# Sending sixteen rows of the first keys ahead of the weights in a GQA decode kernel

## The chip, the cores and the metric

The kernel runs on one core of one Trainium2 chip. The core has five engines that run side by side: TensorE (PE, matmuls; its weight loads are listed apart as PEld), VectorE (DVE), ScalarE (ACT), GpSimd (POOL) and SyncE (SP), and sixteen DMA engines that bring data from the chip's memory (HBM) to the on-chip memory of 128 partitions. The metric is the device time of one execution in microseconds, here the median of several runs. A profile of one execution goes with it; its span runs from the first to the last instruction.

## The reference

One decode step for 8 sequences: the sum of the input, an attention with grouped queries over a cache, and a dense layer with Mish. All data is float32.

```python
xn = _layernorm(x)                                   # x: 8 x 1 x 512
q = (xn @ wq) -> 32 heads of 128                     # wq: 512 x 4096
k, v: 8 x 8 key/value heads x 8192 positions x 128   # four query heads share one
p = softmax(q k^T * 128 ** -0.5);  o = p v
A = o @ wo                                           # wo: 4096 x 512
h = xn @ w1 + b1;  act = h * tanh(softplus(h))       # w1: 512 x 1792
out = x + A + act @ w2                               # w2: 1792 x 512
```

The two caches are 268 MB each; the weights together are some 24 MB. Each byte of a cache is used once.

## The kernel before

The work is cut in 16 packs (`PACKS`): a pack is a pair of key/value heads for two of the eight sequences (`PB`). For each pack and sequence there is one load of keys and one of values, 8 MiB each: 128 rows, one for each partition, of 64 KiB. The host lays the arrays out so that a load is one contiguous stretch of HBM; `rows_of` cuts it into 128 rows.

For each load of keys, PE multiplies it with the expanded queries (`scores`, 64 matmuls into bank `c`); ACT copies the result, PE arranges it in rows, DVE and ACT do the softmax, and one pack later PE multiplies the weights with the values (`values`, into bank `o`). Before all packs there is a part that runs once: `setup` (layer norm of x, small selector tables), `queries` (PE: xn times the first wq, then DVE scales and transposes) and `mish` (xn times w1, then a chain on DVE).

Three places on the chip take the large loads: "a" (tile `kva`, 64 KiB per partition), "b" (`kvb`, 80 KiB) and "w" (`kvw`, 16 KiB). `plan` (line 499) puts a load with its place in a list, `queue`; `pump` (479) takes loads from the head of that list as long as the place of the first one is free, and `release` (491) frees a place when its readers are done and pumps again. So the loads are issued strictly in the order of that list, all of them by SP on one DMA queue. x and b1, both small, are issued by ACT on its own queue. The calls that fill the list are on lines 545 to 571: the first is wq, the second w1 (to place "a"), the third the first keys (to place "b"); then come the second keys (to "a", so after w1's readers), and so on. The first three have places that are free at the start, so SP issues them one after another with no wait.

Each load has a stream, which is the semaphore that its landing raises (`"k0"` for the first keys). Which waits an instruction needs is worked out by `Program` from the tiles that it reads and writes: an instruction on PE that reads a tile written by a load waits for that load's semaphore, with one wait for each semaphore. In the profile nearly all instructions carry line 383, where `issue` emits them, so they are told apart by their tiles: `kvw<-in_wq` is the load of wq, `kva<-in_w` that of w1, `kvb<-in_kT` and `kva<-in_kT` those of keys, `h<-kvw,xnT` the query matmuls, `o<-kva,aT` the first matmuls of mish, `c<-kvb,qT` the scores.

```python
def pump():
    while queue and taken.get(queue[0][1]) in (None, queue[0][0]):
        what, at, load = queue.pop(0)
        taken[at] = what
        landed[what] = load()
```

Of the kernel before, what the change touches and what calls it, by code (L numbers as in the profile page):

```python
# [58 lines left out]
W1R = 2 * CC * P // P  # L59
W2R = G * FT // 2 * FP // P  # L60
FAR = 1e38


ENGINES = ("tensor", "vector", "scalar", "gpsimd", "sync")
# [379 lines left out]
def kernel(  # L444
# [14 lines left out]
    pe, dve, act, pool, sp = (getattr(prog, e) for e in ("tensor", "vector", "scalar", "gpsimd", "sync"))  # L459

    def tile_of(shape, name):
        prog.on_chip.add(name)
        return nc.alloc_sbuf_tensor(name, list(shape), F32).ap()
# [8 lines left out]
    queue = []  # L472
    taken, landed, held = {}, {}, {}

    def rows_of(blocks):

        return blocks.rearrange("j p f -> (j p f)").rearrange("(p f) -> p f", p=P)
# [18 lines left out]
            held[at] = [relay]  # L496
        pump()

    def plan(what, at, blocks, stream, part=(0, 1), lo=0):

        rows = rows_of(blocks)
        n = rows.shape[1]
        t = place[at][:, lo : lo + n]

        cols = slice(round(part[0] * n), round(part[1] * n))

        def load():
            sp.dma_start(t[:, cols], rows[:, cols], stream=stream, to="tensor", after=held.pop(at, ()))
            return t

        queue.append((what, at, load))

    sc = tile_of([P, 512], "sc")
    x_sb = sc[:B, :]
# [6 lines left out]
    def blocks_of(src, p, b):  # L521
        i, k = divmod(p, NP)
        lo = ((k * PB + b) * HKV + 2 * i) * NB
        return src[lo : lo + KN]

    up = [0]

    def plan_k(p, b):
        blocks = blocks_of(kT, p, b)
        if (p, b) == (0, 1):  # L530
            plan(("k", p, b), "a", blocks, "k1")
        else:
            up[0] = KX * BW - up[0]
            plan(("k", p, b), "b", blocks, "k" if p else "k0", lo=up[0])

    def plan_v(p, b, at, stream="v", part=(0, 1)):
        plan(("v", p, b), at, blocks_of(v, p, b), stream, part)

    def plan_wq(i):
        plan(("wq", i), "w", wq[i * CC : (i + 1) * CC], "w")  # L540
# [1 line left out]
    def plan_wo(i, stream="w", part=(0, 1)):  # L542
        plan(("wo", i), "w", wo[i * 4 : i * 4 + 4], stream, part)

    plan_wq(0)
    plan("w1", "a", w1, "w1")
    between = {}
    for i in range(1, PAIRS):
        between[NP * i - 1, 0] = ("wq", i)
# [1 line left out]
    for p in range(PACKS):  # L551
        for b in range(PB):
            plan_k(p, b)
            if (p, b) in between:
                what, i = between[p, b]
                (plan_wq if what == "wq" else plan_wo)(i)
            if p == 1 and b == 0:
                plan_v(0, 0, "a", "v1", (1 / 2, 1))
                plan_v(0, 0, "a", part=(0, 1 / 2))
            elif p > 0:  # L560
                plan_v(p - 1, b, "a")
# [65 lines left out]
    def setup():  # L627
# [63 lines left out]
        dve.reduce_sum(isel, rsel.rearrange("p (i r) -> p i r", i=W4), axis=AX.X)  # L691
        dve.tensor_scalar(far, isel, FAR, -FAR, op0=ALU.mult, op1=ALU.add)
        of_head = tile_of([P, 2, V8], "of_head")
# [365 lines left out]
    for p in range(PACKS):  # L1059
        prog.enter(p)  # L1060
        for b in range(PB):
            k = landed.pop(("k", p, b))
# [44 lines left out]
    p = PACKS - 1  # L1107
# [75 lines left out]
```

## Time and profile before

| what | value |
|---|---|
| median of 3 runs | 1303.62 us (1303.54 to 1303.68) |
| span of the profiled execution | 1302.2 us |
| PE, DVE, ACT, POOL busy | 67%, 30%, 9%, 0% of the span |
| moved by DMA | 561.22 MB, mean 431 GB/s |
| SP's queue (q1) | 99.7% of the 16 engines' span |
| first issue of SP, first score matmul | 0.74 us, 37.66 us |

The profiled execution lies 1.4 us below the runs, because the span leaves out what is before its first and behind its last instruction; its own time is its span beside that. The share of a DMA queue is the time that its packets took, summed over the sixteen engines and divided by sixteen times the stretch; it can pass 100% in a short stretch, because a packet is counted whole where it starts. One packet is one row of a load on one engine, and each load adds one packet of 4 bytes per engine that it runs on, for the semaphore.

### The profile page before, as it was taken

To read this page: it belongs to the slowest core of one execution; us is meant where nothing else is said; L and a number is where in the kernel's file an instruction comes from. 1 tells how busy PE (TensorE), PEld (TensorE's weight loads), DVE (VectorE), ACT (ScalarE), POOL (GpSimd) and SP (SyncE) were. 2 spreads that over 40 slices of the span, in tenths; PEclk is the share of its full clock that TensorE was granted. 3 is DMA by queue.
4 is the path that set the end of the run, shared out by engine and by line. 5 is a ranking of instruction groups with operands and counts; after the bars stand their busy time and mean duration, and the time that the engine had idled before them with its cause. 6 is when DMAs were issued, how large, how long until landed. Compare 5 with 4: busy or idle time off the path is not lost.

```text
span 1302.2 us, 11363 instructions
## 1 busy us (share of the span) xinstructions
PE 869.0 (67%) x4814; PEld 278.5 (21%) x4814; DVE 389.9 (30%) x597; ACT 122.2 (9%) x294; POOL 4.8 (0%) x10
## 2 busy tenths in 40 slices
PE   4786666766567665686656686666866656756568
PEld 1222112212112221122211222111221121212113
DVE  6350504305051230521405132052320515105061
ACT  1020202001020100200102020020100102001020
POOL 1000000000000000000000000000000000000000
PEclk9898789887799788897877897778877888878779
DMA  9999999999999999999999999999999999999998
GB/s 404 447 419 446 421 441 429 431 439 429 439 429 441 425 443 423 436 433 431 439 429 439 420 450 425 441 425 441 429 431 439 429 439 429 441 425 439 427 429 372
DMA packets 11554, 561.22 MB, mean 431 GB/s; under 512 B 1292, under 2 KB 1424, under 8 KB 1688
## 3 DMA queue, kind: packets, MB, share of 16 engines
q1 hardware_dynamic: 11520, 561.06, 99.7%
q8 instruction: 7, 0.11, 0.0%
q10 hardware_dynamic: 24, 0.02, 0.0%
q14 instruction: 3, 0.02, 0.0%
HBM read 561.01 MB, written 0.07 MB: 431 GB/s over the span
## 4 chain that ended last, share of the span: by engine, by line
DMA 61%; PE 31%; DVE 1%; issue 0%; SPq 0%; ACT 0%; DVEq 0%
DMA kvb<-in_kT 60%; PE c L383 29%; DMA kvb<-in_w 2%; PE o L383 1%; DVE raw L383 0%; DVE pt L383 0%; PE h L383 0%; DVE os L383 0%; DVE nm L383 0%; PE s L383 0%; PE m L383 0%; SPq L383 0%; ACT sc L383 0%; DVE acc L383 0%; DVE nr L383 0%
## 5 line engine op out<-in xcount | busy, mean ns | idle before, releaser
L383 PE MATMUL c<-kvb,qT 128*64 128x512 f32 x1984 | 497.7, 665 | 332.8 <-DMA kvb<-in_kT 332.2
L383 PEld LDWEIGHTS c<-kvb,qT 128*64 128x64 f32 x1984 | 160.8, 154 | 669.6 <-issue 459.4
L383 PE MATMUL o<-kva,pt 128*32 128x512 f32 x1984 | 238.0, 635 | 24.5 <-DMA kva<-in_v 24.1
L383 DVE TENSOR_REDUCE nm<-s 128x1 f32<-128x1024 f32 x16 | 19.6, 1225 | 437.0 <-PE s L383 437.0
L383 DVE STREAM_TRANSPOSE raw<-wide 128x2048 f32<-128x2048 f32 x36 | 125.5, 3485 | 19.5 <-ACT wide L383 17.7
L383 ACT COPY sc<-c 128x512 f32<-128x512 f32 x32 | 18.8, 586 | 979.1 <-PE c L383 979.1
L383 PEld LDWEIGHTS o<-kva,pt 128*32 128x32 f32 x1984 | 64.6, 116 | 189.1 <-issue 147.6
L383 ACT ACTIVATE wide<-s,nms 128x512 f32<-128x512 f32 x128 | 88.0, 688 | 130.4 <-DVE nms L383 66.9
L383 DVE TENSOR_TENSOR oT<-m,rt 128x16 f32 (+1 forms) x17 | 3.0, 175 | 229.6 <-PE m L383 229.6
L383 DVE TENSOR_SCALAR os<-o,isel 128x128 f32<-128x128 f32 x32 | 11.2, 350 | 151.1 <-PE o L383 151.1
L383 DVE TENSOR_TENSOR pt<-raw 64x256 f32<-64x256 f32 x128 | 53.6, 418 | 1.9
L383 DVE TENSOR_TENSOR qT<-qc,bsel 128x1024 f32<-128x1024 f32 x34 | 40.2, 1221 | 13.3 <-PE s L383 13.3
L383 PE MATMUL s<-sc,csel 64*128 64x512 f32 x128 | 37.1, 656 | 8.5 <-ACT sc L383 7.1
L383 DVE TENSOR_TENSOR raw<-raw 128x1024 f32<-128x1024 f32 x32 | 39.2, 1225 | 2.9 <-DVE raw L383 0.2
L383 DVE SCALAR_TENSOR_TENSOR os<-o,isel,os 128x128 f32<-128x128 f32 x96 | 33.6, 350 | 3.4
L383 ACT ACTIVATION_READ_ACCUMULATOR wide<-s,nms 128x1 f32 x128 | 24.7, 193 | 0.0
L383 PE MATMUL m<-hsel,os 128*128 128x8 f32 x66 | 12.7, 265 | 10.5 <-DVE lsel L383 10.5
L383 PE MATMUL m<-ident,nm 128*1 128x128 f32 x16 | 4.3, 270 | 21.6 <-DVE nm L383 21.6
L383 PE MATMUL h<-kvw,xnT 128*64 128x512 f32 x64 | 17.6, 700 | 0.0
L383 PE MATMUL c<-kva,qT 128*64 128x512 f32 x64 | 15.7, 652 | 2.1 <-DMA kva<-in_kT 2.1
L383 DVE TENSOR_SCALAR wide<-h 128x512 f32<-128x512 f32 x16 | 11.1, 691 | 19.9 <-PE h L383 19.5
L383 PEld LDWEIGHTS m<-hsel,os 128*128 128x128 f32 x66 | 10.1, 193 | 25.3 <-issue 12.2
(92 smaller groups left out, 162.1 us busy)
## 6 DMA issues: line engine op xcount, KB each, us to landing
kvw<-in_wq SPq DMA_DIRECT2D x4, 2048.0 KB, 30.3
kva<-in_v SPq DMA_DIRECT2D x2, 4096.0 KB, 21.6
kvw<-in_wo SPq DMA_DIRECT2D x3, 2048.0 KB, 30.4
kva<-in_v SPq DMA_DIRECT2D x1, 6144.0 KB, 24.3
kva<-in_w SPq DMA_DIRECT2D x1, 3584.0 KB, 15.8
kva<-in_v SPq DMA_DIRECT2D x1, 2048.0 KB, 28.8
kvb<-in_w SPq DMA_DIRECT2D x1, 2048.0 KB, 13.7
kvw<-in_wo SPq DMA_DIRECT2D x1, 1536.0 KB, 16.9
```

The costliest lines, as they stand in the source:

```text
L383: got = getattr(engine, o.method)(*args, **kw)
```

## The change

`plan` gets an argument `first`: the load that is put in the list then covers only the rows from `first` on, and the rows before it are issued at once, as a DMA of their own with a stream of its own, when `plan` is called. For the first keys `first` is 16. The calls for wq and w1 move behind the call for the first keys, and the rest of the first keys is taken from the head of the list to its end, so that the list begins with wq, w1, keys as before. SP's order of issue is then: rows 0 to 15 of the first keys (16 partitions, 1 MiB), wq, w1, the other 112 rows of the first keys (7 MiB). All other loads stand as they were.

```diff
+AHEAD = 16
...
-    def plan(what, at, blocks, stream, part=(0, 1), lo=0):
+    def plan(what, at, blocks, stream, part=(0, 1), lo=0, first=0):
...
         def load():
-            sp.dma_start(t[:, cols], rows[:, cols], stream=stream, to="tensor", after=held.pop(at, ()))
+            sp.dma_start(t[first:, cols], rows[first:, cols], stream=stream, to="tensor", after=held.pop(at, ()))
             return t
 
         queue.append((what, at, load))
+        if first:
+            sp.dma_start(t[:first], rows[:first], stream=stream + "a", to="tensor")
...
-            plan(("k", p, b), "b", blocks, "k" if p else "k0", lo=up[0])
+            plan(("k", p, b), "b", blocks, "k" if p else "k0", lo=up[0], first=0 if p else AHEAD)
...
-    plan_wq(0)
-    plan("w1", "a", w1, "w1")
     between = {}
...
     for p in range(PACKS):
         for b in range(PB):
             plan_k(p, b)
+            if p == b == 0:
+                plan_wq(0)
+                plan("w1", "a", w1, "w1")
+                queue.append(queue.pop(0))
```

## The prediction

> **What bounds the kernel now.** I read the page first: the busy shares, the strip of forty slices, the queues and the chain that ended last.
>
> ```profile
> PE 869.0 (67%) x4814; PEld 278.5 (21%) x4814; DVE 389.9 (30%) x597; ACT 122.2 (9%) x294; POOL 4.8 (0%) x10
> ...
> DMA  9999999999999999999999999999999999999998
> ...
> DMA packets 11554, 561.22 MB, mean 431 GB/s; under 512 B 1292, under 2 KB 1424, under 8 KB 1688
> ...
> q1 hardware_dynamic: 11520, 561.06, 99.7%
> ...
> DMA 61%; PE 31%; DVE 1%; issue 0%; SPq 0%; ACT 0%; DVEq 0%
> ```
>
> Queue q1, SP's own, carries 561.06 MB and keeps the 16 DMA engines at work for 99.7% of the span. PE's 31% of the chain is a way of following it back: while PE works, the transfers go on. The same view cut to the middle, 38 to 1170 us, leaves out both ends:
>
> ```profile
> DMA packets 9211, 490.26 MB, mean 433 GB/s; under 512 B 1024, under 2 KB 1024, under 8 KB 1024
> ...
> q1 hardware_dynamic: 9208, 490.21, 100.1%
> ```
>
> No gap at all. One engine moves 490.21 MB / 16 / 1132 us = 27.1 GB/s, so **a 64 KiB row takes 2.42 us**, and a load of 128 such rows (8 on each engine) 19.4 us. Nothing can catch up on a queue that is never idle: each microsecond in which an engine of the 16 moves less at the start comes back at the end. So the change is priced at the start of this queue alone. The end of the chain shows the transfers still ahead of PE there:
>
> ```profile
> 1278.36 19.55 DMA kvb<-in_w
> 1297.91 0.04 issue
> 1297.95 1.87 PE h L383 x56
> ```
>
> Next the order of time in the first 40 us:
>
> ```profile
> 0.73 0.61 ACTq L383 DMA_DIRECT2D sc<-in_x  x1
> 0.74 0.38 SPq L383 DMA_DIRECT2D kvw<-in_wq  x1
> 1.18 0.42 SPq L383 DMA_DIRECT2D kva<-in_w  x1
> 1.38 0.25 ACTq L383 DMA_DIRECT2D acc<-in_b  x1
> 1.65 0.42 SPq L383 DMA_DIRECT2D kvb<-in_kT  x1
> ...
> 5.05 0.67 DVE L383 TENSOR_REDUCE st<-sc 8x1 f32<-8x512 f32 x1 [0.91 <-PEq L1142]
> ...
> 10.46 0.22 DVE L383 COPY xnT<-m 128x64 f32<-128x64 f32 x1 [0.80 <-PE m L383]
> ...
> 13.98 6.63 PE L383 MATMUL h<-kvw,xnT 128*64 128x512 f32 x16
> ...
> 21.40 6.20 PE L383 MATMUL o<-kva,aT 128*8 128x448 f32 x64
> ...
> 26.68 2.36 DVE L383 TENSOR_TENSOR qT<-qc,bsel 128x1024 f32<-128x1024 f32 x2
> 27.71 0.33 SPq L383 DMA_DIRECT2D kva<-in_kT  x1
> ...
> 37.66 2.83 PE L383 MATMUL c<-kvb,qT 128*64 128x512 f32 x6 [10.07 <-DMA kvb<-in_kT]
> ```
>
> and, for the tiles kvw, kva and kvb up to 60 us, the times from issue to landing (wq alone; w1 is the least of kva, the first keys the most of kvb):
>
> ```profile
> DMA to landing us min/median/max: 7.7/7.7/7.7
> DMA to landing us min/median/max: 15.8/22.5/29.3
> DMA to landing us min/median/max: 26.7/31.4/36.0
> ```
>
> wq lands at 0.74 + 7.7 = 8.4, w1 at 1.18 + 15.8 = 17.0, the first keys at 1.65 + 36.0 = 37.7: in the order of issue, the 3.67 MB of w1 in 8.6 us. Readers of the weights come later (13.98, 21.40); PE waits 10 us for the keys. Last, the start by queue, in three stretches: 1.70 to 1.79 (x), 1.79 to 3.40, and 5.70 to 6.20 (b1).
>
> ```profile
> q10 hardware_dynamic: 8, 0.02, 178.1%
> ...
> DMA packets 30, 0.36 MB, mean 224 GB/s; under 512 B 8, under 2 KB 8, under 8 KB 8
> ...
> q1 hardware_dynamic: 22, 0.36, 98.3%
> ...
> q10 hardware_dynamic: 4, 0.01, 3.7%
> ```
>
> q1 began at 224 GB/s. The 8 packets of x (8 rows of 2 KiB) took 1.781 x 16 x 0.09 / 8 = 0.32 us each, 4.2 times the 0.076 us of 2 KiB at 27.1 GB/s; the first 22 of wq (16 KiB, over all partitions) 0.983 x 16 x 1.61 / 22 = 1.15 us, 1.9 times their 0.61; the 4 of b1 0.037 x 16 x 0.5 / 4 = 0.074 us, their plain 0.07.
>
> **The change part by part.** No byte is added. *One more issue on SP*: the issue of wq goes from 0.74 to about 1.15 (one issue is 0.38 to 0.42), w1 and the keys likewise; what hides it is the first block, which keeps each ring at work for at least 2.42 us from its start near 1.8. Without that cover it would cost 0.4. One semaphore packet per engine, one more wait of PE ahead of its first score matmul (the block has long landed; only the scores are behind it, and they wait for the other rows anyway) and one more semaphore to clear: nothing to 0.1 us.
>
> *The slow start.* From 1.79 to 3.40 the queue moved 0.36 MB where 433 GB/s would move 0.70: 1.61 x (433 - 224) / 433 = 0.78 us lost. One long row per engine can hide that if it comes of small first packets, and none of it if it is the delay of the first bytes. Bounds of the gain 0 to 0.8; I take **-0.4**, between them.
>
> *Sixteen rows into partitions 0 to 15.* No load of the trace is like this: all big ones cover 128 partitions. If every engine keeps its pace, the block takes 2.42 us and costs nothing, as those rows were due anyway. At the other end, if the sixteen rows come one behind another, it takes 38.7 us. The question is whether neighbouring partitions share a way into the memory. The nearest row is x, eight neighbouring partitions written at once at the start: four times the plain time, while wq, beside it and spread over all partitions, had less than twice. b1, also narrow, shows no slowing, but its packets fill 0.30 us of a 0.5 us stretch, so they hardly met. I go by x, as the row that is nearest in shape and time, and take 4 rows to a way: 4 x 2.42 = **9.7 us** in place of 2.42. The queue is served in order, so wq, w1 and all after them are late by the difference: **+7.3** (bounds 0 and +36).
>
> [...]
>
> *The other 112 rows.* Spread evenly they are 7 to an engine, 16.9 us at full pace. [...] Bounds 0 (the ways don't bind) and +17; I take two and a half row times, **+6.0**, nearer the low end, since the meetings of engines at different steps should partly pass each other. The lag of the slowest engine counts, because each landing waits for all sixteen, and it stays, because every later load gives each engine the same bytes.
>
> *What is late next.* With +9.3 at the front (9.7 - 0.4), wq lands near 17.7, so the queries go from 13.98 to 17.7 and mish from 21.40 to about 26.3; k1's issue goes from 27.71 to about 32.6, while the ring still holds the first keys past 45. The query operands, done at 29.04, come 3.7 later, still ahead of the keys. x and b1, on ACT's queue, could get behind the long rows: x is asked for at 5.05, and its chain ends at 10.68 (10.46 + 0.22); were x late by as much as 7 us, that would be covered by wq's landing at 17.7. So it is the lag of the queue alone that reaches the end.
>
> Sum: -0.4 + 7.3 + 6.0 = **+12.9**. Against the execution's own span, 1302.2 + 12.9 = 1315.1; what lies around the span is 1303.62 - 1302.2 = 1.4, so the forecast is **1316.5** against the median of 1303.62.
>
> **The rivals.** *No shared way.* The engines set 27.1 GB/s, not the place written; x was slow only because it was first, as wq's first packets were too, and b1's plain time speaks for this. Then wq lands 2.4 us later, at 10.8, ahead of its reader at 13.98, w1 at 19.4, ahead of 21.40, the keys no later: 1303.6 - 0.4 = 1303.2, from 1302.8 (the whole slow start won back) to 1304. It decides if the block lands by about 5 us. Against it stands x beside wq. Faster by more than 0.2% has no source: 0.8 us is all that the start holds, unless the first packets also come earlier by some of the 1.0 us between the issue at 0.74 and 1.79, in all 1.8 of the 2.6 needed.
>
> *The block alone is slow.* The four ways are shared, but the 112 rows meet so little, or the engines that leave the block early fill the idle ways, that only 7.3 stays: 1303.6 + 7.3 - 0.4 = 1310.5.
>
> *Much worse.* The sixteen rows go to one engine (the change then doesn't do what it says): 36.3 later, 1339.5. Or the 112 rows go out sixteen neighbours at a time, so that each of seven steps meets like the block: 7 x 7.3 = 51 more, 1361. Full-width loads keep 433 GB/s, so that ordering isn't what the queue does with 128 rows. [...]
>
> **How the numbers follow.** About 0.2% (2.6 us) is what can be told from no change. Forecast, shared ways with meetings in the 112 rows: 0.58, with its own range 1312.5 (9.7 - 0.8, no meetings beyond the eighth row) to 1322 (7.3 + 11). Block alone: 0.10. Much worse: 0.06. No shared way: 0.24 within 0.2%, and 0.02 for faster. So slower 0.74, same 0.24, faster 0.02. The range must take in the case of no change, as leaving it and the worst out would leave out more than 2 in 10: low 1302.8, high 1322; above lies the worst case and a few in 100 of the forecast.
>
> **What would show it.** After the change the timeline has the keys' small issue first, then wq, w1, keys. If I am right, the stretch from about 2 to 11 us moves little over 1 MiB, near 110 GB/s; wq lands past 17 instead of at 8.4; PE's first score matmul starts near 50 instead of 37.66; the middle keeps 433 GB/s and the difference at 50 us is the difference at the end. If wq lands near 11 and the scores start at 37 to 38, there is no shared way and I am wrong in the sign. If wq lands late but the scores are only 7 later, the 112 rows are overpriced; if the middle falls below 433 GB/s, or the lag at the first scores is not that of the end, the claim that the queue alone sets the time is wrong.

## The result, and the profile after

The kernel after takes 1324.8 us (median of 5 runs, 1324.48 to 1326.22) against 1303.58 us before (5 runs, 1303.48 to 1303.68): ratio 1.0164, 95% interval 1.0153 to 1.0176. It is 21.2 us slower. The forecast was slower by 12.9, with 1322.0 as the top of the range: the sign was right, the size too small.

The page of the kernel after, the rows that answer to those of before:

```profile
GB/s 270 313 422 434 438 428 434 434 432 434 438 428 434 438 428 434 438 428 434 438 430 432 438 430 432 438 425 436 440 428 432 442 424 434 442 430 432 438 426 360
DMA packets 11570, 561.22 MB, mean 424 GB/s; under 512 B 1308, under 2 KB 1440, under 8 KB 1704
...
q1 hardware_dynamic: 11536, 561.06, 99.7%
...
DMA 62%; PE 33%; another core or an unknown queue 2%; DVE 2%; issue 0%; SPq 0%; ACT 0%; DVEq 0%
```

The bytes are the same and q1 is still counted as at work for 99.7% of a longer span, because a packet that is held up counts as work (in the table below, 1.79 to 11.20 us has a share of 1.10 at 139 GB/s). The loss stands in the first two of the forty slices (33 us each), 270 and 313 GB/s; from the third on all is as it was. The middle alone, 62 to 1190 us, by queue:

```profile
DMA packets 9185, 488.63 MB, mean 433 GB/s; under 512 B 1022, under 2 KB 1022, under 8 KB 1022
...
q1 hardware_dynamic: 9181, 488.57, 100.2%
```

433 GB/s, as before the change. In order of time, the start:

```profile
0.74 0.39 SPq L384 DMA_DIRECT2D kvb<-in_kT  x1
1.18 0.41 SPq L384 DMA_DIRECT2D kvw<-in_wq  x1
...
1.64 0.68 SPq L384 DMA_DIRECT2D kva<-in_w  x1
2.37 0.44 SPq L384 DMA_DIRECT2D kvb<-in_kT  x1
...
5.79 0.67 DVE L384 TENSOR_REDUCE st<-sc 8x1 f32<-8x512 f32 x1 [0.92 <-PEq L1147]
...
17.58 5.75 PE L384 MATMUL h<-kvw,xnT 128*64 128x512 f32 x16 [2.79 <-DMA kvw<-in_wq]
...
26.19 6.20 PE L384 MATMUL o<-kva,aT 128*8 128x448 f32 x64 [1.99 <-DMA kva<-in_w]
...
32.50 0.34 SPq L384 DMA_DIRECT2D kva<-in_kT  x1
...
59.10 3.68 PE L384 MATMUL c<-kvb,qT 128*64 128x512 f32 x8 [26.71 <-DMA kvb<-in_kT]
```

and for tiles kvw and kvb up to 70 us the times from issue to landing (wq; then the block of 16 rows as the least and the 112 rows as the most):

```profile
DMA to landing us min/median/max: 16.4/16.4/16.4
DMA to landing us min/median/max: 12.0/34.4/56.7
```

The block lands at 0.74 + 12.0 = 12.7, wq at 17.6 (8.4 before), w1 at 26.1 (it is asked for at 26.19, where it is waited for), the 112 rows at 2.37 + 56.7 = 59.1 (37.7 before). PE's first score matmul moves from 37.66 to 59.10, by 21.4 us, and the end of the span by 21.3 (1302.2 to 1323.5). What is lost by the first scores is the whole loss.

Where it goes shows in a table of stretches of the kernel after; the last two columns are the share of the DMA engines (a packet counted whole where it starts) and GB/s. The first row is the block; then the starts of the seven steps that the 112 rows take (one row per engine in each step); the last is the whole of the 112 rows:

```profile
1.79:11.20 9.41, 0.62 (x4) 0.55 (x4) 5.50 (x19) 2.77 (x3) 0.64 (x3) 1.00 1.10 139
25.00:25.60 0.60, 0.00 (x0) 0.00 (x0) 0.60 (x1) 0.00 (x0) 0.00 (x0) 1.00 7.46 1748
29.30:30.50 1.20, 1.20 (x20) 0.34 (x14) 1.17 (x2) 0.00 (x0) 0.00 (x0) 1.00 4.01 881
34.10:35.60 1.50, 0.00 (x0) 0.00 (x0) 1.07 (x3) 0.40 (x1) 0.00 (x0) 0.97 1.83 666
37.10:38.30 1.20, 0.00 (x0) 0.00 (x0) 1.16 (x3) 0.00 (x0) 0.00 (x0) 0.50 2.39 819
39.70:42.00 2.30, 0.00 (x0) 0.00 (x0) 2.27 (x2) 0.00 (x0) 0.00 (x0) 0.50 1.90 456
43.70:46.50 2.80, 0.00 (x0) 0.00 (x0) 1.36 (x3) 0.00 (x0) 0.00 (x0) 0.50 1.68 374
48.30:51.20 2.90, 0.00 (x0) 0.00 (x0) 0.00 (x0) 0.00 (x0) 0.00 (x0) 0.50 1.62 362
25.00:58.00 33.00, 6.20 (x64) 1.66 (x64) 18.12 (x23) 0.58 (x1) 0.00 (x0) 0.66 1.05 277
```

Where 16 packets start in a stretch, their mean time is share x width. The first and second step: 7.46 x 0.60 = 4.5 us and 4.01 x 1.20 = 4.8 us, each in place of 2.42. The third and the fourth (15 packets each) are 1.83 x 1.50 x 16 / 15 = 2.9 and 2.39 x 1.20 x 16 / 15 = 3.1, the fifth 1.90 x 2.30 = 4.4, the sixth 1.68 x 2.80 = 4.7, the seventh 1.62 x 2.90 = 4.7. So five steps take nearly twice their time, and two not much more than their own. By the trace's packets fifteen engines end their seventh row at 53.5 to 55.7 us; one, a row behind from the third step on, ends it at 58.0, and the landing waits for that one. Why it fell behind isn't shown.

### The profile page after: what moved, and what is told of

Its sections match the earlier page's. It is cut to its first block, busy times and chain, and to the rows that moved or that the text cites. A ratio compares the mean times of both kernels' runs of the same rounds, so it can differ in the third digit from the quotient of the medians.

```text
span 1323.5 us, 11364 instructions
## 1 busy us (share of the span) xinstructions
PE 872.5 (66%) x4814; PEld 279.7 (21%) x4814; DVE 389.9 (29%) x597; ACT 122.1 (9%) x294; POOL 4.8 (0%) x10
## 3 DMA queue, kind: packets, MB, share of 16 engines
q1 hardware_dynamic: 11536, 561.06, 99.7%
## 4 chain that ended last, share of the span: by engine, by line
DMA 62%; PE 33%; another core or an unknown queue 2%; DVE 2%; issue 0%; SPq 0%; ACT 0%; DVEq 0%
DMA kvb<-in_kT 56%; PE c L384 30%; PE o L384 3%; DMA kva<-in_v 3%; DMA kva<-in_w 2%; DMA kvb<-in_w 1%; DVE raw L384 1%; DVE pt L384 0%; DVE os L384 0%; PE m L384 0%; PE h L384 0%; PE s L384 0%; SPq L384 0%; DVE nm L384 0%
## 5 line engine op out<-in xcount | busy, mean ns | idle before, releaser
L384 DVE STREAM_TRANSPOSE raw<-wide 128x2048 f32<-128x2048 f32 x36 | 125.4, 3482 | 19.5 <-ACT wide L384 17.7
L384 DVE TENSOR_SCALAR os<-o,isel 128x128 f32<-128x128 f32 x32 | 11.2, 350 | 152.4 <-PE o L384 152.4
L384 PE MATMUL m<-hsel,os 128*128 128x8 f32 x66 | 12.7, 265 | 10.5 <-DVE lsel L384 10.5
```

The source lines that it names most:

```text
L384: got = getattr(engine, o.method)(*args, **kw)
```

## Experiments

Three theories were held against each other. W: neighbouring partitions share ways into the on-chip memory, so that rows which are written at the same time by one way (rows that meet) hold each other up. S: neighbouring rows share something in HBM, where they are read. O: the order or the number of the loads is at fault, the weights being late.

**p1_probes: the time of a load by itself.** Before all other loads, nine loads into the place of the first keys, each behind the landing of the one ahead. (In the text `bt` is that place, 128 x 16384, `src` the first keys.)

```diff
+    PROBES = [(bt, src), (bt[0:16], src[0:16]), (bt[0::8], src[0:16]), (bt[0:16], src[0::8]),
+        (bt[0:64], src[0:64]), (bt[32:96], src[0:64]), (bt[16:128], src[16:128]),
+        (bt[:, : KR * BW // 8], src[:, : KR * BW // 8]), (bt, src)]
+    for i, (dst, rows_in) in enumerate(PROBES):
+        last = [sp.dma_start(dst, rows_in, stream=f"probe{i}", to="sync", after=last)]
...
     prog.enter(0)
```

Left out here, and in e4, e5 and p2, is a change to `Program`, by which it works out the partitions of a place with a stride.

> Before all other loads SP issues nine loads of the first keys one after another, each waiting for the landing of the one ahead of it, so that the time from issue to landing of each stands by itself; the usual loads follow and the result is unchanged. Let f be what a landing costs beside the rows (the full load of 128 rows takes 19.4 us of rows, so f is its time less 19.4; about 2 us by wq, which took 7.7 us for 4.9 us of rows). Theory W (the ways into the on-chip memory are shared by neighbouring partitions): rows 0-15 into partitions 0-15 take about 8.5 to 9.7 + f; the same 16 rows into every eighth partition much less, 2.4 to 4.8 + f; 16 rows from every eighth place of HBM into partitions 0-15 as long as the first, 8.5 to 9.7 + f. Theory S (neighbouring rows share something where they are read): the second as long as the first, the third 2.4 + f. 64 rows into partitions 0-63 against the same 64 rows into 32-95: by W the two differ if ways repeat within a half of the partitions, by S they are equal. [...] The 112 rows into partitions 16-127 alone: 16.9 + f if their meeting other loads made the delay, up to 33 + f if they delay themselves. One eighth of the columns of all partitions, also 1 MiB: 2.4 to 2.7 + f under W and S alike.

This kernel ran once, as did that of p2; only stretches of their traces are used. One row for each probe, from the first packet's start to the last one's end (the trace's packets set the edges; last column GB/s):

```profile
1.80:22.50 20.70, 1.63 (x12) 1.47 (x12) 9.11 (x34) 2.77 (x3) 4.42 (x5) 1.00 0.96 406
23.70:33.40 9.70, 0.00 (x0) 0.00 (x0) 0.00 (x0) 0.00 (x0) 0.00 (x0) 1.00 0.88 108
36.00:41.60 5.60, 0.00 (x0) 0.00 (x0) 0.00 (x0) 0.00 (x0) 0.00 (x0) 1.00 0.81 187
43.40:53.00 9.60, 0.00 (x0) 0.00 (x0) 0.00 (x0) 0.00 (x0) 0.00 (x0) 1.00 0.88 109
55.30:76.30 21.00, 0.00 (x0) 0.00 (x0) 0.00 (x0) 0.00 (x0) 0.00 (x0) 1.00 0.96 200
78.30:89.20 10.90, 0.00 (x0) 0.00 (x0) 0.00 (x0) 0.00 (x0) 0.00 (x0) 1.00 0.94 385
90.30:121.40 31.10, 0.00 (x0) 0.00 (x0) 0.00 (x0) 0.00 (x0) 0.00 (x0) 1.00 0.95 236
123.30:126.80 3.50, 0.00 (x0) 0.00 (x0) 0.00 (x0) 0.00 (x0) 0.00 (x0) 1.00 0.85 300
128.00:148.80 20.80, 0.00 (x0) 0.00 (x0) 0.00 (x0) 0.00 (x0) 0.00 (x0) 1.00 1.00 421
```

Rows 2 to 4 are 1 MiB in 16 rows: 9.7 us into partitions 0 to 15; 5.6 us for the same source into every eighth partition; 9.6 us into 0 to 15 again from every eighth row of HBM. The place written sets the time, not the place read. This is as W has it, and S falls. Rows 5 and 6 are the same 64 rows of HBM, on as many engines (shares 0.96 and 0.94 of the sixteen): 21.0 us into partitions 0 to 63, 10.9 us into 32 to 95. Row 7: the 112 rows take 31.1 us all by themselves, where full pace is 16.9; their delay needs no other load. Row 8: 1 MiB over all partitions takes 3.5 us, even with packets of 8 KiB. Rows 1 and 9, all 128 rows, take 20.7 and 20.8 us where full pace is 19.4: some 1.3 us of the time of a lone load are its two ends. By place the pace is so 108 GB/s into 0 to 15, 187 into every eighth partition, 200 into 0 to 63, 385 into 32 to 95 and 236 into 16 to 127. What W's ways are, and which partitions share one, no run shows.

**e1_cols: the same MiB cut by columns.**

```diff
-AHEAD = 16
+AHEAD = KR * BW // 8
...
-            sp.dma_start(t[:first], rows[:first], stream=stream + "a", to="tensor")
+            sp.dma_start(t[:, :first], rows[:, :first], stream=stream + "a", to="tensor")
```

with the later load taking the columns from `first` on.

> As the change, with the first MiB cut the other way: the first eighth of each of the 128 rows (8 KiB each) goes ahead of wq and w1, the other seven eighths behind them. Same bytes, same order, same two loads. If the cut by partitions is the cause: as before the change, 1303.2 to 1304.0 us. If the cause is the order (the weights come later, or one more load on the queue): slower by some of the 21 us. If the slow start of small packets was worth gaining, it isn't gained here, as these packets are smaller still: not below 1303.2.

1303.56 us against 1303.71, ratio 1.0002 (0.9993 to 1.0011): the time of before. A MiB of keys ahead of the weights costs nothing that shows when it covers all partitions, though wq lands later there too (at 10.7 us, before 8.4). O falls.

**e2_behind: the cut alone, nothing moved.** In the kernel before, the first keys stay third in the list and are issued as two loads.

```diff
         def load():
+            if what == ("k", 0, 0):
+                sp.dma_start(t[:16], rows[:16], stream=stream + "a", to="tensor")
+                sp.dma_start(t[16:], rows[16:], stream=stream, to="tensor", after=held.pop(at, ()))
+                return t
```

> The kernel before, with the first keys cut in 16 rows and 112 rows where they stood, behind wq and w1; nothing is moved ahead. If the cut by partitions is the cause: 1323 to 1326 us, as the change, since the queue is as late by the end of the first keys; wq and w1 land as before (8.4 and 17.0 us). If moving ahead of the weights is the cause: 1303.6.

1325.41 us against 1303.71, ratio 1.0165 (1.0149 to 1.0180): the whole loss, with wq and w1 as early as before. The first score matmul of that kernel:

```profile
59.36 3.31 PE L383 MATMUL c<-kvb,qT 128*64 128x512 f32 x8 [32.60 <-DMA kvb<-in_kT]
```

**e3_w1_first: does the slow start hang on the size of the first packets?**

```diff
-    plan_wq(0)
-    plan("w1", "a", w1, "w1")
+    plan("w1", "a", w1, "w1")
+    plan_wq(0)
```

> The kernel before with w1 (28 KiB rows) issued ahead of wq (16 KiB rows). Asks whether the slow start of the queue depends on the size of the first packets, as the change supposes. If it does, the queue is ahead by 0.2 to 0.5 us at the first keys and the end: 1303.1 to 1303.4. If the first bytes are slow whatever their packet: 1303.6. The queries start some 3 us later, which the first keys cover.

1303.95 us against 1303.71, ratio 1.0001 (0.9992 to 1.0010). The first scores start at 37.24 in its trace, 0.4 earlier than before, but nothing of it is left in the time. A gain below 0.1% is not excluded; none shows.

**e4_block_then_all and e5_spread_then_all: the block without the 112 rows, in two places.** The load behind the weights covers all 128 rows, so the 16 rows are read twice (1 MiB more, 2.42 us at full pace). In e4 the block goes to partitions 0 to 15, in e5 to every fourth partition from 32 to 92.

```diff
-            sp.dma_start(t[first:, cols], rows[first:, cols], ...
+            sp.dma_start(t[:, cols], rows[:, cols], ...
...
-            sp.dma_start(t[:first], rows[:first], stream=stream + "a", to="tensor")
+            sp.dma_start(t[:first], rows[:first], stream=stream + "a", to="sync")      # e4
+            sp.dma_start(t[32:93:4], rows[:first], stream=stream + "a", to="sync")     # e5
```

> As the change, with all 128 rows in the later load in place of 112 (the 16 rows are read twice, 1 MiB more, 2.42 us at full pace). Takes the term of the 112 rows away and keeps the block. If the block costs 9.6 us and the 112 rows the rest: 1303.7 + 9.6 = 1313.3, less up to 0.5. If the 112 rows cost nothing and the block all of it: 1323 to 1327.

> As the run with the block and then all 128 rows, but the 16 rows ahead go to every fourth partition from 32 to 92 (and are written over later). Same bytes, packets, engines and order. If the places alone set the price: 1303.7 + 2.4 = 1306.1, less up to 0.5 if the long first rows win some of the slow start. If sixteen long rows ahead are slow wherever they go: 1313.

e4: 1312.84 us against 1303.61, ratio 1.0071 (1.0054 to 1.0088). e5: 1306.26, ratio 1.0020 (1.0011 to 1.0030). Both move the same bytes in the same packets on the same engines in the same order. Their start, e4 and then e5 (e5's in two stretches):

```profile
1.79:11.20 9.41, 0.62 (x4) 0.55 (x4) 6.25 (x23) 2.77 (x3) 1.10 (x4) 1.00 1.08 136
```

```profile
1.79:4.80 3.01, 0.00 (x0) 0.00 (x0) 1.50 (x6) 0.00 (x0) 0.20 (x1) 1.00 0.96 350
4.80:11.20 6.40, 0.61 (x4) 0.55 (x4) 4.36 (x15) 2.77 (x3) 0.51 (x3) 1.00 0.97 414
```

Without the doubled 2.42 us the block costs 9.2 - 2.4 = 6.8 us in partitions 0 to 15 and 2.65 - 2.4 = 0.2, nothing that can be told, when spread. So of the change's 21.2 us the block is 6.8 and the 112 rows 14.4; the probe of these alone gave 31.1 - 16.9 = 14.2, of which some 1.3 are the ends of a lone load. And e5 answers what a long first row for each engine is worth when it is not held up: no gain shows.

**e6_middle_half: another cut by partitions, where the first keys stand.**

```diff
+            if what == ("k", 0, 0):
+                for i, (lo_p, hi_p) in enumerate(((32, 96), (0, 32), (96, 128))):
+                    sp.dma_start(t[lo_p:hi_p], rows[lo_p:hi_p], stream=stream + "abc"[i], to="tensor")
+                return t
```

> The kernel before with the first keys cut by partitions where they stand: 32-95 in one load, then 0-31, then 96-127. [...] 4 x 2.7 = 10.8: 1314.5. If any cut by partitions costs as the change: 1324. [...]

1314.77 us against 1303.61, ratio 1.0086 (1.0069 to 1.0102): 11.2 us. The forecast of 10.8 was the author's estimate: no loss in 32 to 95, which took 10.9 us in p1, and in the two outer quarters 5.1 us a step in place of 2.42, two steps each, about the pace of 0 to 63 (21.0 us for four steps, the ends included). That 96 to 127 goes at this pace was not shown by a probe. The price of a cut follows from the places, not from there being a cut: these three loads cost 11.2 us, the two of e2 21.7.

**p2_probes: are a few of sixteen rows slowed, or all of them?**

```diff
+    PROBES = [(bt, src)] + [(bt[at : at + 15 * by + 1 : by], src[0:16]) for at, by in
+        ((32, 4), (28, 4), (24, 4), (20, 4), (36, 4), (7, 7), (18, 7), (16, 7), (0, 7), (11, 7))]
```

> As the probes before: a full load, then ten loads of the same 16 rows of 64 KiB, each behind the landing of the one ahead, all before the usual loads. Only the places change: every fourth partition from 32, 28, 24, 20 and 36, then every seventh from 7, 18, 16, 0 and 11. [...]

For each of the ten a stretch of 2 us in which its 16 packets start (524 GB/s says that it is all of them), so that their mean time is share x 2.00:

```profile
24.00:26.00 2.00, 0.00 (x0) 0.00 (x0) 0.00 (x0) 0.00 (x0) 0.00 (x0) 1.00 1.43 524
29.20:31.20 2.00, 0.00 (x0) 0.00 (x0) 0.00 (x0) 0.00 (x0) 0.00 (x0) 1.00 1.50 524
36.40:38.40 2.00, 0.00 (x0) 0.00 (x0) 0.00 (x0) 0.00 (x0) 0.00 (x0) 1.00 2.32 524
44.00:46.00 2.00, 0.00 (x0) 0.00 (x0) 0.00 (x0) 0.00 (x0) 0.00 (x0) 1.00 2.16 524
50.90:52.90 2.00, 0.00 (x0) 0.00 (x0) 0.00 (x0) 0.00 (x0) 0.00 (x0) 1.00 1.54 524
58.20:60.20 2.00, 0.00 (x0) 0.00 (x0) 0.00 (x0) 0.00 (x0) 0.00 (x0) 1.00 1.52 524
65.40:67.40 2.00, 0.00 (x0) 0.00 (x0) 0.00 (x0) 0.00 (x0) 0.00 (x0) 1.00 1.51 524
72.60:74.60 2.00, 0.00 (x0) 0.00 (x0) 0.00 (x0) 0.00 (x0) 0.00 (x0) 1.00 2.20 524
79.80:81.80 2.00, 0.00 (x0) 0.00 (x0) 0.00 (x0) 0.00 (x0) 0.00 (x0) 1.00 2.29 524
87.10:89.10 2.00, 0.00 (x0) 0.00 (x0) 0.00 (x0) 0.00 (x0) 0.00 (x0) 1.00 1.37 524
```

The means are 2.9, 3.0, 4.6, 4.3, 3.1 us for every fourth partition from 32, 28, 24, 20 and 36, and 3.0, 3.0, 4.4, 4.6, 2.7 for every seventh from 7, 18, 16, 0 and 11. By the trace's packets there are three cases. From 32 by four and 11 by seven all sixteen packets take 2.4 to 3.2 us. From 28 and 36 by four, 7 and 18 by seven, two of the sixteen take 4.1 to 4.7 us and the other fourteen 2.4 to 3.4. From 24 and 20 by four, 16 and 0 by seven, all sixteen take 3.9 to 5.2. Read by W, the two slow rows of the second case are a pair that meets; which rows would meet in the third, and why all are slowed there, is not shown.

## Why the prediction was right and wrong

*What bounds the kernel*: right. The lag at the first scores, 21.4, is the lag at the end, 21.3, with 433 GB/s between them; e2 and e4 add that the place of the delay in the queue doesn't matter (1325.41 us with the cut behind the weights, 1324.8 with the block ahead of them; the block alone, ahead of them in e4, costs 9.2 with its 2.42 of bytes).

*The slow start, -0.4*: no gain could be measured. With packets of 8 KiB first (e1), of 28 KiB (e3) and of 64 KiB spread over partitions 32 to 92 (e5) the time stays within 0.3 us of what the bytes ask. The loss of 0.78 us in the first stretch is there in the rows of before, but larger first packets did not win it back; what makes it is not shown. The value taken lay within its bounds of 0 to 0.8 and the nearer one was 0.

*Sixteen rows into partitions 0 to 15, 9.7 us in place of 2.42, +7.3*: right. The probe took 9.7, and e4 gives the term with the slow start in it as 6.8, where the prediction had 7.3 - 0.4 = 6.9. The first 9.4 us show 139 GB/s and not the forecast 110, as engines that were done with their row had begun wq (its first packet starts at 9.65 us). Going by the fourfold time of x's eight packets was partly luck: x was at the slow start of the queue as well, and no run separates the two in it.

*The other 112 rows, +6.0*: this is the step that failed in size. That neighbouring rows of these 112 would meet on their way was the author's estimate; no run shows such a meeting as such, nor the 2.4 us of an eighth row in the range's low end (9.7 is 7.3 + 2.4). What the runs show in its place is 14.4 us (alone 14.2, or 12.9 without the ends of a lone load), above the 11 that the range allowed for the term and near the upper bound of 17, seven row times. The prediction took the low side because engines that meet at different steps should partly pass each other, and nearly all of them do not: in the first step of the 112 rows all sixteen packets took 4.2 to 4.6 us, in the second 4.7 to 5.1. The trace of the change has means of 4.5, 4.8, 2.9, 3.1, 4.4, 4.7, 4.7 us for the seven steps. Let each engine have seven neighbouring rows, engine i (0 to 15) those from partition 16 + 7i. Two of p2's probes are then two of these steps: every seventh partition from 16 is the first (mean 4.4, here 4.5), from 18 the third (3.0, here 2.9). The other five have no probe. Where all sixteen packets are held up alike, the engines stay in step, and fifteen of them go on so to the end of the load. The seven steps make 29 us, 12 over full pace, and the landing then waits for the one engine that is a row behind. The first score matmul, forecast near 50, came at 59.10: this term's 8.4 us above its forecast. That each engine has seven neighbouring rows is inferred from the agreement in these two steps; the profile doesn't name the engine of a packet. With a few of the sixteen rows slowed in a step, as in the fourth (two at 4.4 and 4.5 us, thirteen at 2.8 to 3.0), the low value was natural; what was not known is that in five of the seven steps all of them would be.

*What is late next*: right to 0.2 us in all but one. wq was forecast to land at 17.7 and landed at 17.6, mish at 26.3 and ran at 26.19, k1's issue at 32.6 and came at 32.50; none of it reached the end. The query operands came 2.7 us later (29.04 to 31.78), not 3.7, and well ahead of the keys all the same. The setup starts 0.74 us later (x is first read at 5.79, before 5.05), more than the 0.4 of one issue, and is covered by wq's lateness as argued.

*The rivals*: "no shared way" falls with e1, e4 and e5; "the block alone is slow" with the 14.4 us of the 112 rows; "much worse" with the probes, as a MiB took 9.7 us and not 38.7, and no step of the 112 rows took the time of four rows.

## What to carry to other kernels

On a queue that is always full, price a change in a load by the partitions that it covers. Here a load cut by columns left the kernel's time as it was (300 GB/s for a lone MiB, its ends included). Loads cut by partitions ran alone at anything from 108 to 385 GB/s, and the same bytes on as many engines differed by nearly two (108 and 187, 200 and 385). If a load has to be cut by partitions, compare where the rows that are written at the same time lie: 32 to 95 took 10.9 us, 0 to 63 took 21.0, and 16 to 127 ran nearly as badly as these (236 GB/s against 200), though only sixteen partitions are left out there. In this kernel, whose queue is never idle, such a delay came out at the end in full (21.4 us at the first scores, 21.3 at the end).

## What the runs showed of the hardware that was not expected

Sixteen rows of 64 KiB written at the same time, one on each engine, were in some places slowed all together. In four of p2's ten probes all sixteen packets took 3.9 to 5.2 us (means 4.3 to 4.6), against 2.4 to 3.2 in the two undisturbed ones (means 2.7 and 2.9); in the other four only two packets were slow, at 4.1 to 4.7 us (means 3.0 to 3.1). The rows from 28 and from 24, by four each, lie four partitions apart, and their means are 3.0 and 4.6 us. In the steps of the 112 rows both stand beside each other: all sixteen packets at 4.2 us and more in the first two, two of them in the fourth. What holds up the others in the slow places was not found; no run separates it, and it stays open.
